# Scores behind values, and the gate products of two tiles in one go, in a fused attention and expert kernel

## The chip, the core and the metric

The kernel runs on one core of a Trainium2 chip. The metric is the time of one execution on the device, in microseconds (us); smaller is better. The program is one launch, and the tensors lie in device memory before it starts and after it ends.

## What is computed

Three stages follow each other: attention within chunks of 64 positions, a dense layer pair with a clipped activation, and a layer of 8 experts of which each token uses two. The token order of the second and third stage is batch, position; their width of 512 is 8 heads of 64. Cut to what matters:

```python
# q, k, v: (4, 8, 576, 64); chunks of 64 positions, so 9 chunks for each head
scores = q_c @ k_c.T / 8
attn = exp(scores - scores.max(-1)); attn /= attn.sum(-1) + 1e-9
x = (attn @ v_c) -> (2304 tokens, 512)

h = x @ w_in                              # 512 -> 2048
x = (h * clip(h + 3, 0, 6) / 6) @ w_out   # 2048 -> 512

logits = x @ w_gate + log1p(exp(x @ w_noise)) * noise      # 8 experts
top2 = the two largest; weights = softmax over the two
out[token] = sum over its two experts: weight * (relu(x @ w1[e]) @ w2[e])   # 512 -> 1024 -> 512
```

Everything is fp32 in and out. The large products are made exact enough by splitting each operand into a rounded high part and a low rest; three matmuls (high by high, high by low, low by high) stand for one.

## The kernel before

The 2304 tokens are 18 tiles of 128. The dense stage takes them in five blocks of 4, 3, 4, 4 and 3 tiles, and goes through 16 weight units for each block. In the profile's times block 0 ends at about 124 us, block 1 at 203, block 2 at 302 and block 3 at 398; the change is in blocks 1, 2 and 3.

Within a unit `u` TensorE (PE) does first S1 (L294: 12 matmuls, the input by this unit's `w_in`, one column for each token of the block) and then S2 of the unit before it (L304: 3 matmuls for each tile of the block that is added up). Between S1 and S2 of the same unit lie two operations of ScalarE (ACT) and two of VectorE (DVE), which make the clipped activation and split it (L329, L330, L331, L336). A unit of S2 thus has the length of one S1 and one S2 as slack.

Besides these matmuls a block carries small work for its neighbours:

- attention for the tiles of the block after it. For one tile: scores on PE (`att_sc`, L197, 16 products of 64x64, shown as 32 matmuls), maximum and subtraction on DVE (L205, L211), exponential on ACT (L223), sum and normalisation on DVE (L228 to L235), transposes on PE (`att_pt`, L247), a copy on ACT (L251), values on PE (`att_xo`, L264, again 16 products of 64x64), and the split into high and low (L274 on ACT, L277 on DVE).
- the gate for the tiles of the block before it. For one tile: four reads of its rows from device memory into `xq` (`gate_l`, L380, issued by SyncE, SP), a transposition on DVE (`gate_d`, L372), a product with the gate weights on PE (`gate_mm`, L413), a copy on ACT (`gate_lp`, L418), a transpose on PE (`gate_rt`, L425) and a sum on DVE (`gate_rr`, L432). After all tiles of a block follow the choice of two experts and the positions.

Scores, transposes and values of attention use the middle 512 columns of a pair of PSUM banks (`middle`, 256 columns in each bank); the gate uses the two outer strips of 256 (`ENDS`) in blocks 2 and 3, and a bank of its own (`p5`) in block 1, where only three tiles are added up.

The order on PE, DVE and ACT is written out by hand: `between` makes lists of what is done at which unit, `at(B, u, f, t)` puts f behind the activation of unit u, and `s1_(u, k, ...)` and `s2_(u, k, ...)` put it behind the k-th third of S1 or the k-th tile of S2 on PE. DVE and ACT get their instructions in the order in which this code issues them, and each engine does them strictly in that order. SP, which issues all plain transfers, is not in that list: a scheduler orders its queue by its own estimates, and SP too goes through it in order.

A further piece of SP's queue: `zero_out` (L739) fills the output and a part of the table `x2d` with zeros: five transfers of 1536 KB that SP issues. It is called in unit 8 of block 2, but the scheduler places it in SP's queue early in block 1, since it waits for little.

The tiles `xq` come from a pool of three buffers (tag `x2`), which is also where the block's results (`x2`) lie until they are written to `x2d`. `gate_d` writes into a fixed tile, `at_[1]`.

Of the kernel before, what the change touches and what calls it, by code (L numbers as in the profile page):

```python
# [8 lines left out]
F32 = mybir.dt.float32  # L9
# [4 lines left out]
AF = mybir.ActivationFunctionType  # L14
ALU = mybir.AluOpType
# [4 lines left out]
P = 128  # L20
NT = 2304
DM = 512
KD = DM // P
# [5 lines left out]
B0 = [sum(BT[:b]) for b in range(len(BT))]  # L29
# [23 lines left out]
def tile_kernel(ctx, tc, qkv, w1u, w2u, wg, noise, out):  # L53
# [15 lines left out]
               "p3": (3, 0), "p4": (3, 1)}  # L69

    def middle(pair):
        return pairs[pair][:, 2 * P:6 * P]
# [19 lines left out]
    early = const.tile([P, NE], F32, name="early")  # L92
    quarter = const.tile([P, 1], F32, name="quarter")
    wg_sb = const.tile([P, KD, 32], F32, name="wg_sb")
    lp = const.tile([P, P], F32, name="lp")
    noise_sb = const.tile([P, NTILE, NE], F32, name="noise_sb")
    pay = const.tile([P, NTILE, 2, 2], I32, name="pay")
    cnt = const.tile([P, NE + 1], I32, name="cnt")
# [88 lines left out]

    def att_sc(t, pair=0):  # L190
        qt, kt, vt = st["qkv", t]
        sc = middle(pair).rearrange("p (r h k) -> p r h k", r=2, h=KD)
        for hp in range(KD):
            for c in range(2):
                for r in range(2):
                    s = slice(r * 64, r * 64 + 64)
                    nc.tensor.matmul(sc[c * 64:c * 64 + 64, r, hp, :], qt[s, hp, c, :], kt[s, c, hp, :],  # L197
                                     start=True, stop=True)
        st["sc", t] = sc

    def att_mx(t, acts):
        sc = st["sc", t]
        mx = work.tile([P, 8, 1], F32, tag="mx", bufs=3, name="mx")
        sc = sc.rearrange("p r h k -> p (r h) k")
        nc.vector.tensor_reduce(mx, sc, axis=AX.X, op=ALU.max)  # L205
        sm = (lead[t][:, 3 * DM:] if t < BT[0] else arena[:, 6]).rearrange("p (h k) -> p h k", h=8)
        su = work.tile([P, 8, 1], F32, tag="su", bufs=3, name="su")
        if acts:
            nc.vector.tensor_scalar(mx, mx, -0.125, None, op0=ALU.mult)
        else:  # L210
            nc.vector.tensor_tensor(sm, sc, mx.to_broadcast([P, 8, 64]), op=ALU.subtract)  # L211
            st.pop(("sc", t))
        st["att", t] = (sm, su, mx, acts)

    def att_e(t, heads=range(8)):
        sm, su, mx, acts = st["att", t]
# [25 lines left out]

    def att_pt(t, pair=0):
        sm = st.pop(("att", t))[0].rearrange("p h k -> p (h k)")
        pt = middle(pair)
# [8 lines left out]
    def att_xo(t, pair=0):  # L254
        at = st.pop(("attT", t))
        qt, kt, vt = st.pop(("qkv", t))

        xo = middle(pair).rearrange("p (a j n) -> p a j n", a=2, j=2)
        for c in range(2):
            for j in range(2):  # L260
                for a in range(2):
                    s = slice(a * 64, a * 64 + 64)
                    for r in range(2):
                        nc.tensor.matmul(xo[r * 64:r * 64 + 64, a, j, c * 64:c * 64 + 64], vt[s, c, j, r, :],  # L264
                                         at[s, r * 2 + j, c * 64:c * 64 + 64], start=True, stop=True)
        st["xo", t] = xo
# [113 lines left out]
            nc.sync.dma_start(xq[32 * a:32 * a + 32].rearrange("p (c n) -> p c n", c=KD), rows[a])  # L380
        st["xq", t] = xq

    def gate_d(t, i=1):
        x = at_[i].rearrange("p k n -> p (k n)")
        quarters_t(x, st.pop(("xq", t)))
        st["x2T", t] = x.rearrange("p (c b j) -> p b c j", c=KD, b=KD)

# [14 lines left out]
    ENDS = [pairs[0][:, :2 * P], pairs[0][:, 6 * P:]]  # L402

    def gate_m(t, tag="p6"):
        gate_mm(t, tag)
        gate_lp(t)

    def gate_mm(t, tag="p6"):

        xt = st.pop(("x2T", t))  # L410
        lg = bank(tag, [P, P], "lg")
        for kd in range(KD):
            nc.tensor.matmul(lg[32 * kd:32 * kd + 32].rearrange("p (c j) -> p c j", c=KD), wg_sb[:, kd, :], xt[:, kd],  # L413
                             start=True, stop=True, tile_position=(0, 32 * kd))
        st["lg", t] = lg

    def gate_lp(t):
        nc.scalar.activation(lp, st.pop(("lg", t)), AF.Copy)  # L418

    def gate_r(t, tag="p6"):  # L420
        gate_rt(t, bank(tag, [P, P], "lt"))
        gate_rr(t)

    def gate_rt(t, lt):
        nc.tensor.transpose(lt, lp, ident)  # L425
        st["lt", t] = lt

    def gate_rr(t):
# [3 lines left out]
        nc.vector.tensor_reduce(st["lgs", g][:, t - GRP[g][0], :], st.pop(("lt", t)).rearrange("p (k e) -> p e k", k=KD)[:, :16],  # L432
                                axis=AX.X, op=ALU.add)

    def small(shape, name, dt=F32, bufs=1):
# [337 lines left out]
    def at(d, u, f, *a):  # L773
        d.setdefault(u, []).append((f, *a))
# [10 lines left out]
    def regular(b, side, A={}, B={}, Z={}):  # L785
        nonlocal prev
        for u in range(U1):
            mlp_s1(b, u, gtile(), 0)
            run(Z.get(u, []))
            mlp_act(b, u)  # L790
            run(A.get(u, []))
            for pb, v in prev:
                mlp_o(pb, v)
            mlp_lo(b, u)
            for pb, v in prev:
                if v == U1 - 1:
                    x2_out(pb)
            run(B.get(u, []))
            if b == NB - 1 and u > 0:
                pump()  # L800
            run(side.get(u, []))
            prev = [(b, u)]

    def between(b, attn, gates, top, per):


        A, B, Z, nt, n0 = {}, {}, {}, BT[b], st.get("tick", 0)
        before = BT[b - 1]

        def s2_(u, k, f, *a):  # L810
            n = n0 + 3 + k if u == 0 else n0 + 3 + before + (3 + nt) * (u - 1) + 3 + k
            at(ticks, n, f, *a)

        def s1_(u, k, f, *a):
            n = n0 + k if u == 0 else n0 + 3 + before + (3 + nt) * (u - 1) + k
            at(ticks, n, f, *a)


        for i, u in enumerate(gates):
            t = B0[b - 1] + i  # L820
            at(B, max(u - 2, 0), gate_l, t)
            at(B, u - 1, gate_d, t)
            if nt > 3:
                s2_(u, nt, gate_mm, t)
                at(B, u, gate_lp, t)
                s1_(u + 1, 2, gate_rt, t, ENDS[0][:, P:])
                s1_(u + 1, 2, gate_rr, t)
            else:
                s1_(u + 1, 1, gate_mm, t, "p5")
                at(A, u + 1, gate_lp, t)  # L830
                s1_(u + 2, 1, gate_rt, t, bank("p5", [P, DM], "lt")[:, P:2 * P])
                s1_(u + 2, 1, gate_rr, t)
        for i, u in enumerate(attn):
            t = B0[b + 1] + i
            s2_(u, 1, att_sc, t)
            at(B, u, att_mx, t, False)
            at(B, u, att_e, t)
            at(B, u + 1, att_n, t)
            if nt > 3:
                s1_(u + 2, 3, att_pt, t)  # L840
                at(A, u + 2, att_at, t, at_[0])
                s2_(u + 2, nt, att_xo, t)
                end = (B, u + 2)
            else:
# [12 lines left out]
        at(B, pm, gate_ps, b - 1)  # L857
        return A, B, Z
# [94 lines left out]
    ends = ctx.enter_context(tc.tile_pool(name="ends", bufs=1, space=PSUM, side="right", reuse_waits="tile"))  # L953
    single.update((tag, ends.tile([P, DM], F32, name="b" + tag)) for tag in ("p6", "p7"))
# [139 lines left out]
```

## Time and profile before

| | us |
|---|---|
| three runs | 935.14, 935.76, 937.75 (median 935.76) |
| the profiled execution | 934.58 |
| its span, first to last instruction | 932.8 |
| PE busy in the span | 913.1 |
| DVE busy | 482.2 |
| ACT busy | 333.2 |

Busy PE is not PE at its peak: the records of matmuls overlap. What a piece of PE's work costs is therefore read from starts, from the start of one row of the timeline to the start of the next. All such differences below are made so. DMA sizes in the profile are in KB of 1024 bytes, and a transfer's time to landing is from its issue by SP until its semaphore is set.

### The profile page before, as it was taken

The page shows a single profiled execution, that of the slowest core. Times are in us where ns is not written, and L with a number is a line of the kernel's source. Part 1 is how long each engine was busy: PE and PEld are TensorE (multiplying, and loading weights), DVE is VectorE, ACT ScalarE, POOL GpSimd, SP SyncE. Part 2 cuts the span into 40 slices and gives each one's busy share as a digit, 9 for nine tenths or more (in the row PEclk, how much of TensorE's full clock was granted, in tenths as well). Part 3 has the DMA queues.
Part 4 walks back from the last instruction along what each step waited for, and adds up shares of the span by engine and source line. Part 5 has one row for each costly group of instructions (what it writes and reads, how often), then busy time and mean ns, then how long its engine had stood idle before and what let it go on. Part 6 is the DMA issues. An engine that isn't in the chain of part 4 may idle for free.

```text
span 932.8 us, 14436 instructions
## 1 busy us (share of the span) xinstructions
PE 913.1 (98%) x5814; PEld 766.3 (82%) x5814; DVE 482.2 (52%) x912; ACT 333.2 (36%) x643; POOL 231.9 (25%) x213
## 2 busy tenths in 40 slices
PE   6999999999999999999999999999999999999996
PEld 3677788887777777788988898898988889888885
DVE  6999965454454443537543555444545454441311
ACT  5565433333233322344541443333434333321210
POOL 0000000030002000033203345754645445332321
PEclk9999999999999999999999999999999999999999
DMA  9636639113112410024541764653746355240422
GB/s 342 204 112 193 193 98 372 61 37 101 35 34 58 136 35 1 1 69 113 156 139 15 191 145 116 151 121 113 145 117 128 111 128 127 69 54 20 54 25 33
DMA packets 49916, 101.49 MB, mean 109 GB/s; under 512 B 17040, under 2 KB 23056, under 8 KB 49840
## 3 DMA queue, kind: packets, MB, share of 16 engines
q1 hardware_dynamic: 38736, 80.38, 27.4%
q0 software_dynamic: 11104, 20.10, 11.9%
q8 instruction: 47, 0.77, 0.4%
q14 instruction: 29, 0.24, 0.1%
HBM read 77.66 MB, written 22.75 MB: 108 GB/s over the span
## 4 chain that ended last, share of the span: by engine, by line
PE 86%; DVE 10%; ACT 2%; issue 1%; DMA 0%; POOL 0%; POOLq 0%; DVEq 0%; ACTq 0%
PE bp L304 41%; PE bp L294 40%; DVE u L171 2%; DVE u L163 2%; DVE u L162 1%; DVE r L330 1%; DVE w L185 1%; DVE g L336 1%; PE pair L197 1%; PE pair L264 1%; PE pair L247 1%; ACT w L178 1%; PE bp L581 0%; ACT r L329 0%; DMA xr<-x2d,tab 0%
## 5 line engine op out<-in xcount | busy, mean ns | idle before, releaser
L304 PE MATMUL bp<-w,g 128*128 128x512 f32 (+1 forms) x1812 | 453.9, 396 | 0.4 <-ACT g L331 0.3
L304 PEld LDWEIGHTS bp<-w,g 128*128 128x128 f32 (+1 forms) x1812 | 328.3, 185 | 73.7 <-DVE g L336 0.8
L294 PE MATMUL bp<-Xa,w 128*128 128x304 f32 (+3 forms) x1344 | 244.2, 332 | 2.3 <-ACT w L178 1.9
L294 PEld LDWEIGHTS bp<-Xa,w 128*128 128x128 f32 x1344 | 209.0, 188 | 30.4 <-ACT w L178 5.2
L554 POOL DMA_INDIRECT xrq<-x2d,iq x114 | 119.5, 1048 | 95.7 <-DVE iq L548 34.4
L597 DVE SCALAR_TENSOR_TENSOR g<-bp,g 128x304 fp32r<-128x304 f32 (+2 forms) x128 | 60.4, 472 | 130.9 <-ACT g L596 130.9
L139 DVE TENSOR_TENSOR w<-raw,w 128x1024 fp32r<-128x1024 f32 x64 | 78.4, 1226 | 89.0 <-ACT w L138 89.0
L519 POOL DMA_INDIRECT table<-pay,slot x36 | 36.3, 1009 | 338.9 <-DVE slot L516 247.9
L596 ACT ACTIVATE g<-bp 128x304 fp32r<-128x304 f32 (+2 forms) x128 | 54.3, 424 | 168.6 <-PE bp L294 168.5
L294 PE MATMUL bp<-Xb,w 128*128 128x384 f32 (+1 forms) x480 | 106.1, 366 | 0.0
L294 PE MATMUL bp<-Xe,w 128*128 128x304 f32 (+1 forms) x672 | 102.7, 308 | 0.0
L294 PEld LDWEIGHTS bp<-Xe,w 128*128 128x128 f32 x672 | 99.8, 188 | 3.3
L330 DVE SCALAR_TENSOR_TENSOR r<-r,bp 128x512 f32<-128x512 f32 (+1 forms) x80 | 50.6, 632 | 91.8 <-ACT r L329 91.6
L294 PEld LDWEIGHTS bp<-Xb,w 128*128 128x128 f32 x480 | 85.3, 188 | 12.5 <-issue 1.8
L624 POOL DMA_INDIRECT out_dram<-arena,tab x40 | 62.7, 1567 | 123.5 <-DVE arena L621 100.1
L329 ACT ACTIVATE r<-bp,b 128x512 f32<-128x512 f32 (+1 forms) x80 | 51.3, 642 | 106.4 <-PE bp L294 106.4
L138 ACT ACTIVATE w<-raw 128x1024 fp32r<-128x1024 f32 x64 | 67.7, 1058 | 58.8 <-PE bp L304 58.5
L336 DVE TENSOR_TENSOR g<-r,g 128x512 fp32r<-128x512 f32 (+1 forms) x80 | 51.0, 637 | 40.2 <-ACT g L331 40.2
L331 ACT ACTIVATE g<-r 128x512 fp32r<-128x512 f32 (+1 forms) x80 | 47.2, 590 | 60.3 <-DVE r L330 60.3
L178 ACT ACTIVATE w<-u 128x512 fp32r<-128x512 f32 x32 | 20.3, 633 | 32.5 <-DVE u L171 32.5
L372 DVE STREAM_TRANSPOSE arena<-xrq 128x512 f32<-128x512 f32 (+1 forms) x30 | 31.4, 1046 | 0.1
L735 POOL MEMSET zero<- 128x1024 f32 x1 | 1.0, 952 | 115.1 <-DVE u L171 115.1
(148 smaller groups left out, 483.8 us busy)
## 6 DMA issues: line engine op xcount, KB each, us to landing
raw<-in_w2u_dram SPq DMA_DIRECT2D x64, 512.0 KB, 4.0
raw<-in_w1u_dram SPq DMA_DIRECT2D x24, 512.0 KB, 4.9
arena<-in_qkv_dram SPq DMA_DIRECT2D x14, 768.0 KB, 4.1
out_dram<-zero SPq DMA_DIRECT2D x4, 1536.0 KB, 19.4
rawx<-in_w1u_dram SPq DMA_DIRECT2D x8, 512.0 KB, 8.4
x2d<-x SPq DMA_DIRECT2D x15, 256.0 KB, 3.4
xq<-x2d SPq DMA_DIRECT2D x44, 64.0 KB, 3.4
xrq<-x2d,iq POOLq DMA_INDIRECT x114, 2.6
```

The costliest lines, as they stand in the source:

```text
L138: nc.scalar.activation(w[:, 0], raw, AF.Copy)
L139: nc.vector.tensor_tensor(w[:, 1], raw, w[:, 0].bitcast(F32), op=ALU.subtract)
L294: nc.tensor.matmul(dst, w[:, a, kd * P:(kd + 1) * P], x[:, b, kd, t0:t0 + n], start=(k == 0), stop=(k == 3 * KD - 1))
L304: nc.tensor.matmul(acc[i][:gi.shape[2]], gi[:, a], w[:, b, DM:], start=(first and j == 0), stop=(last and j == 2))
L329: nc.scalar.activation(r, st["h", b], AF.Relu, bias=b3)
L330: nc.vector.scalar_tensor_tensor(r, r, 6.0, st["h", b], op0=ALU.min, op1=ALU.mult)
L331: nc.scalar.activation(st["g", b, u][:, 0], r, AF.Copy)
L336: nc.vector.tensor_tensor(g[:, 1], st["r", b], g[:, 0].bitcast(F32), op=ALU.subtract)
L554: nc.gpsimd.indirect_dma_start(out=xr[:, c * P:(c + 1) * P], out_offset=None, in_=x2q, in_offset=bass.IndirectOffsetOnAxis(ap=st["iq", key ...
L596: nc.scalar.activation(g[:, 0, t0:t0 + n], h, AF.Relu)
L597: nc.vector.scalar_tensor_tensor(g[:, 1, t0:t0 + n], h, 0.0, g[:, 0, t0:t0 + n].bitcast(F32), op0=ALU.max, op1=ALU.subtract)
L624: s = nc.gpsimd.indirect_dma_start(out=out, out_offset=bass.IndirectOffsetOnAxis(ap=tab[:n, i, 0:1], axis=0), in_=y, in_offset=None, compu ...
```

## The change

Scores get a place of their own, the two outer strips of the pair (`outer`), so that they can follow the values of the tile before directly. The two operations on DVE that read them take a view of two strips. In blocks 1 to 3 attention starts every 3 (block 1) or 2 units (blocks 2 and 3), so that the values of one tile and the scores of the next but one step fall on the same place. The gate takes a list of one or two tiles: products of both, one copy, transposes of both, one sum. `gate_d` writes a tile from the pool `x2` in place of `at_[1]`. The tables at the end set the units.

```diff
+    def outer(pair):
+        return pairs[pair].rearrange("p (r n) -> p r n", r=4)[:, ::3]
...
-    lp = const.tile([P, P], F32, name="lp")
+    lp = const.tile([P, 2 * P], F32, name="lp")
...
-    def att_sc(t, pair=0):
+    def att_sc(t, pair=0, place=middle):
         qt, kt, vt = st["qkv", t]
-        sc = middle(pair).rearrange("p (r h k) -> p r h k", r=2, h=KD)
+        sc = place(pair).rearrange("p r (h k) -> p r h k", h=KD)
...
-    def gate_d(t, i=1):
-        x = at_[i].rearrange("p k n -> p (k n)")
+    def gate_d(t):
+        x = work.tile([P, DM], F32, tag="x2", bufs=3, name="xT")
         quarters_t(x, st.pop(("xq", t)))
...
+    def gate_mm(ts, lg):
+        for i, t in enumerate(ts):
+            xt = st.pop(("x2T", t))
+            for kd in range(KD):
+                nc.tensor.matmul(lg[32 * kd:32 * kd + 32, i * P:(i + 1) * P].rearrange("p (c j) -> p c j", c=KD),
+                                 wg_sb[:, kd, :], xt[:, kd], start=True, stop=True, tile_position=(0, 32 * kd))
+        st["lg", ts[0]] = lg[:, :len(ts) * P]
+
+    def gate_lp(ts):
+        nc.scalar.activation(lp[:, :len(ts) * P], st.pop(("lg", ts[0])), AF.Copy)
...
+    def gate_rt(ts, lt):
+        for i in range(len(ts)):
+            nc.tensor.transpose(lt[:, i * P:(i + 1) * P], lp[:, i * P:(i + 1) * P], ident)
+        st["lt", ts[0]] = lt[:, :len(ts) * P]
...
-        for i, u in enumerate(gates):
-            t = B0[b - 1] + i
-            at(B, max(u - 2, 0), gate_l, t)
-            at(B, u - 1, gate_d, t)
+        first = B0[b - 1]
+        for u, n in gates:
+            ts = list(range(first, first + n))
+            first += n
+            for i, t in enumerate(ts):
+                at(B, u - n - 1 + i, gate_l, t)
+                at(B, u - n + i, gate_d, t)
             if nt > 3:
-                s2_(u, nt, gate_mm, t)
-                at(B, u, gate_lp, t)
-                s1_(u + 1, 2, gate_rt, t, ENDS[0][:, P:])
-                s1_(u + 1, 2, gate_rr, t)
+                s2_(u, nt, gate_mm, ts, ENDS[0])
+                at(B, u, gate_lp, ts)
+                s1_(u + 1, 2, gate_rt, ts, ENDS[1])
+                s1_(u + 1, 2, gate_rr, ts)
             else:
-                s1_(u + 1, 1, gate_mm, t, "p5")
...
+                p5 = bank("p5", [P, DM], "lg")
+                s1_(u + 1, 1, gate_mm, ts, p5)
...
         for i, u in enumerate(attn):
             t = B0[b + 1] + i
-            s2_(u, 1, att_sc, t)
+            if nt > 3:
+                s2_(u, nt, att_sc, t, 0, outer)
+            else:
+                s1_(u, 2, att_sc, t, 0, outer)
...
-        regular(1, {}, *between(1, (1, 4, 8, 12), (3, 5, 7, 9), 11, 2))
+        regular(1, {}, *between(1, (1, 4, 7, 10), ((4, 2), (8, 2)), 11, 2))
...
-        regular(2, side, *between(2, (1, 4, 8, 12), (5, 7, 9), 10, 2))
+        regular(2, side, *between(2, (1, 3, 5, 7), ((4, 2), (8, 1)), 10, 2))
...
-        regular(3, side, *between(3, (2, 6, 11), (3, 5, 7, 9), 10, 1))
+        regular(3, side, *between(3, (1, 3, 5), ((4, 2), (8, 2)), 10, 1))
```

What this does on PE in block 1, units 4 and 5. Before (`bp4`, `bp3` take S1; `bp0`, `bp1`, `bp2` take S2; `pair0` the attention; `bp5` the gate):

```order
L294 MATMUL bp4_428<-Xb_99,w_586 128x384 x4
L413 MATMUL bp5_424<-at1_101,wg_sb_87 32x128 x4
L294 MATMUL bp4_428<-Xb_99,w_586 128x384 x4
L264 MATMUL pair0_72<-at0_100,arena_94 64x64 x16
L294 MATMUL bp4_428<-Xb_99,w_586 128x384 x4
L304 MATMUL bp0_425<-w_536,g_1442 128x512 x3
L197 MATMUL pair0_72<-arena_94 64x64 x16
L304 MATMUL bp1_426<-w_536,g_1442 128x512 x3
L304 MATMUL bp2_423<-w_536,g_1442 128x512 x3
L294 MATMUL bp3_427<-Xb_99,w_656 128x384 x4
L425 MATMUL bp5_424<-ident_78,lp_88 128x128
L294 MATMUL bp3_427<-Xb_99,w_656 128x384 x8
```

The same place with the change (lines are numbered anew: 297 is S1, 307 S2, 267 the values, 200 the scores, 415 the gate product):

```order
L297 MATMUL bp4_428<-Xb_99,w_586 128x384 x8
L267 MATMUL pair0_72<-at0_100,arena_94 64x64 x16
L200 MATMUL pair0_72<-arena_94 64x64 x16
L297 MATMUL bp4_428<-Xb_99,w_586 128x384 x4
L307 MATMUL bp0_425<-w_536,g_1448 128x512 x3
L307 MATMUL bp1_426<-w_536,g_1448 128x512 x3
L307 MATMUL bp2_423<-w_536,g_1448 128x512 x3
L297 MATMUL bp3_427<-Xb_99,w_656 128x384 x4
L415 MATMUL bp5_424<-xT_1437,wg_sb_87 32x128 x4
L415 MATMUL bp5_424<-xT_1479,wg_sb_87 32x128 x4
L297 MATMUL bp3_427<-Xb_99,w_656 128x384 x8
```

The scores moved behind the values, the first tile's gate product moved from unit 4 to unit 5, and the second tile's stands right behind it.

On DVE, units 2 to 4 of block 1, before (`at1` from `xq_1400` is `gate_d` of the first tile; `r` and `g` belong to S1 and S2):

```order
L372 STREAM_TRANSPOSE at1_101<-xq_1400 128x512
L228 TENSOR_REDUCE su_1407<-arena_94 128x8
L229 TENSOR_SCALAR su_1407<-su_1407 128x8
L230 RECIPROCAL su_1407<-su_1407 128x8
L235 TENSOR_TENSOR arena_94<-arena_94,su_1407 128x512
L330 SCALAR_TENSOR_TENSOR r_1455<-r_1455,bp3_427 128x384
L336 TENSOR_TENSOR g_1442<-r_1455,g_1442 128x384
L277 TENSOR_TENSOR Xa_95<-pair0_72,Xa_95 128x2x2x128
L330 SCALAR_TENSOR_TENSOR r_1515<-r_1515,bp4_428 128x384
```

With the change:

```order
L375 STREAM_TRANSPOSE xT_1437<-xq_1400 128x512
L231 TENSOR_REDUCE su_1407<-arena_94 128x8
L232 TENSOR_SCALAR su_1407<-su_1407 128x8
L233 RECIPROCAL su_1407<-su_1407 128x8
L238 TENSOR_TENSOR arena_94<-arena_94,su_1407 128x512
L333 SCALAR_TENSOR_TENSOR r_1461<-r_1461,bp3_427 128x384
L339 TENSOR_TENSOR g_1448<-r_1461,g_1448 128x384
L375 STREAM_TRANSPOSE xT_1479<-xq_1439 128x512
L280 TENSOR_TENSOR Xa_95<-pair0_72,Xa_95 128x2x2x128
L333 SCALAR_TENSOR_TENSOR r_1530<-r_1530,bp4_428 128x384
```

The transposition of the second tile (`xq_1439`) now stands one row behind unit 3's split, ahead of unit 4's activation.

On SP, from the writing of block 0's results on, before (`xq` with its numbers are the four tiles of block 0, `zero` the fill):

```order
L360 DMA x2d_76<-x2e_1354 128x512
L380 DMA xq_1400<-x2d_76 32x4x128 x4
L380 DMA xq_1473<-x2d_76 32x4x128 x4
L380 DMA xq_1582<-x2d_76 32x4x128 x4
L739 DMA x2d_76<-zero_2491 384x1x1024
L739 DMA out_0_dram<-zero_2491 128x3x1024 x4
L380 DMA xq_1677<-x2d_76 32x4x128 x4
L119 DMA arena_94<-in_qkv_dram 128x1536 x4
```

With the change:

```order
L363 DMA x2d_76<-x2e_1354 128x512
L383 DMA xq_1400<-x2d_76 32x4x128 x4
L745 DMA x2d_76<-zero_2550 384x1x1024
L745 DMA out_0_dram<-zero_2550 128x3x1024 x4
L383 DMA xq_1439<-x2d_76 32x4x128 x4
L122 DMA arena_94<-in_qkv_dram 128x1536
L383 DMA xq_1585<-x2d_76 32x4x128 x4
L383 DMA xq_1631<-x2d_76 32x4x128 x4
```

The reads of the second tile moved from ahead of the five fills to behind them, and the fills moved up by eight reads.

## Rows read from the trace of the kernel before

**Rows 1.** Profile page: busy time of the span, and the chain by engine.
```profile
PE 913.1 (98%) x5814; PEld 766.3 (82%) x5814; DVE 482.2 (52%) x912; ACT 333.2 (36%) x643; POOL 231.9 (25%) x213
...
PE 86%; DVE 10%; ACT 2%; issue 1%; DMA 0%; POOL 0%; POOLq 0%; DVEq 0%; ACTq 0%
```

**Rows 2.** Timeline of PE, block 1: start us, busy us, line, tiles, shape.
```profile
133.79 2.25 PE L294 MATMUL bp<-Xb,w 128*128 128x384 f32 x12
135.88 2.25 PE L304 MATMUL bp<-w,g 128*128 128x512 f32 x9
...
143.14 0.86 PE L294 MATMUL bp<-Xb,w 128*128 128x384 f32 x4
...
146.62 0.85 PE L304 MATMUL bp<-w,g 128*128 128x512 f32 x3
147.40 0.69 PE L197 MATMUL pair<-arena 64*64 64x64 f32 x32
148.03 1.67 PE L304 MATMUL bp<-w,g 128*128 128x512 f32 x6
149.53 0.86 PE L294 MATMUL bp<-Xb,w 128*128 128x384 f32 x4
150.23 0.27 PE L425 MATMUL bp<-ident,lp 128*128 128x128 f32 x1
150.25 1.64 PE L294 MATMUL bp<-Xb,w 128*128 128x384 f32 x8
151.73 2.25 PE L304 MATMUL bp<-w,g 128*128 128x512 f32 x9
153.81 0.86 PE L294 MATMUL bp<-Xb,w 128*128 128x384 f32 x4
154.61 0.42 PE L413 MATMUL bp<-at,wg_sb 128*32 128x128 f32 x8
154.96 1.66 PE L294 MATMUL bp<-Xb,w 128*128 128x384 f32 x8
156.46 0.85 PE L304 MATMUL bp<-w,g 128*128 128x512 f32 x3
```

**Rows 3.** Timeline of PE at the start: two tiles' scores in a row.
```profile
10.13 1.16 PE L197 MATMUL pair<-lead 64*64 64x64 f32 x64
```

**Rows 4.** Timeline of SP in block 1: issues, start and length of each stretch.
```profile
130.63 5.74 SPq L380 DMA_DIRECT2D xq<-x2d  x12
136.47 1.71 SPq L739 DMA_DIRECT2D x2d<-zero  x1
138.22 4.51 SPq L739 DMA_DIRECT2D out_dram<-zero  x4
142.83 7.95 SPq L380 DMA_DIRECT2D xq<-x2d  x4
```

**Rows 5.** Profile page, DMA issues: engine, count, KB each, us to landing.
```profile
out_dram<-zero SPq DMA_DIRECT2D x4, 1536.0 KB, 19.4
```

**Rows 6.** DMA packets by size, first from 143 to 158 us, then from 158 to 162.
```profile
DMA packets 1504, 5.98 MB, mean 398 GB/s; under 512 B 48, under 2 KB 48, under 8 KB 1503
...
DMA packets 756, 1.15 MB, mean 287 GB/s; under 512 B 80, under 2 KB 592, under 8 KB 756
```

**Rows 7.** Timeline of DVE in block 1: start us, busy us, line, operation.
```profile
138.37 1.10 DVE L372 STREAM_TRANSPOSE at<-xq 128x512 f32<-128x512 f32 x1
...
142.26 0.56 DVE L336 TENSOR_TENSOR g<-r,g 128x384 fp32r<-128x384 f32 x1 [0.59 <-ACT g L331]
...
169.25 1.08 DVE L372 STREAM_TRANSPOSE at<-xq 128x512 f32<-128x512 f32 x1
```

**Rows 8.** Windows after PE's last matmul: busy PE, PEld, DVE, ACT, POOL, clock, DMA.
```profile
923.80:928.60 4.80, 0.00 (x0) 0.00 (x0) 0.75 (x1) 0.00 (x0) 2.66 (x2) 1.00 0.67 80
928.70:932.80 4.10, 0.00 (x0) 0.00 (x0) 0.00 (x0) 0.00 (x0) 0.00 (x0) 0.50 0.17 31
```

**Rows 9.** Timeline of PE, the first matmuls of the program.
```profile
1.07 3.17 PE L679 MATMUL pair<-ones 128*128 128x512 bf16 x7 [1.07 <-DVE early L704]
4.27 1.13 PE L197 MATMUL pair<-lead 64*64 64x64 f32 x32
```

More of the change, by code (lines that the diff above doesn't have):

```diff
@@ L71, in middle @@
     def middle(pair):
-        return pairs[pair][:, 2 * P:6 * P]
+        return pairs[pair][:, 2 * P:6 * P].rearrange("p (r n) -> p r n", r=2)
+    def outer(pair):
+        return pairs[pair].rearrange("p (r n) -> p r n", r=4)[:, ::3]
     def bank(tag, shape, name):
@@ L202, in att_mx @@
         sc = st["sc", t]
-        mx = work.tile([P, 8, 1], F32, tag="mx", bufs=3, name="mx")
-        sc = sc.rearrange("p r h k -> p (r h) k")
+        mx = work.tile([P, 2, KD, 1], F32, tag="mx", bufs=3, name="mx")
         nc.vector.tensor_reduce(mx, sc, axis=AX.X, op=ALU.max)
@@ L210, in att_mx @@
         else:
-            nc.vector.tensor_tensor(sm, sc, mx.to_broadcast([P, 8, 64]), op=ALU.subtract)
+            nc.vector.tensor_tensor(sm.rearrange("p (r h) k -> p r h k", r=2), sc, mx.to_broadcast([P, 2, KD, 64]),
+                                    op=ALU.subtract)
             st.pop(("sc", t))
-        st["att", t] = (sm, su, mx, acts)
+        st["att", t] = (sm, su, mx.rearrange("p r h o -> p (r h) o"), acts)
     def att_e(t, heads=range(8)):
@@ L244, in att_pt @@
         sm = st.pop(("att", t))[0].rearrange("p h k -> p (h k)")
-        pt = middle(pair)
+        pt = middle(pair).rearrange("p r n -> p (r n)")
         for m in range(KD):
@@ L256, in att_xo @@
         qt, kt, vt = st.pop(("qkv", t))
-        xo = middle(pair).rearrange("p (a j n) -> p a j n", a=2, j=2)
+        xo = middle(pair).rearrange("p a (j n) -> p a j n", j=2)
         for c in range(2):
@@ L404, in gate_m, with gate_rr @@
     def gate_m(t, tag="p6"):
[L405 to L418, printed above, removed]
-    def gate_r(t, tag="p6"):
[L421 to L428, printed above, removed]
+        gate_mm([t], bank(tag, [P, P], "lg"))
+        gate_lp([t])
+    def gate_mm(ts, lg):
[7 more added lines that the diff above has]
+        nc.scalar.activation(lp[:, :len(ts) * P], st.pop(("lg", ts[0])), AF.Copy)
+    def gate_r(t, tag="p6"):
+        gate_rt([t], bank(tag, [P, P], "lt"))
+        gate_rr([t])
+    def gate_rt(ts, lt):
+        for i in range(len(ts)):
+            nc.tensor.transpose(lt[:, i * P:(i + 1) * P], lp[:, i * P:(i + 1) * P], ident)
+        st["lt", ts[0]] = lt[:, :len(ts) * P]
+    def gate_rr(ts):
+        t, n = ts[0], len(ts)
         g = max(i for i in range(len(GRP)) if GRP[i][0] <= t)
@@ L431, in gate_rr @@
             st["lgs", g] = small([P, 5, 16], "lgs")
-        nc.vector.tensor_reduce(st["lgs", g][:, t - GRP[g][0], :], st.pop(("lt", t)).rearrange("p (k e) -> p e k", k=KD)[:, :16],
+        i = t - GRP[g][0]
+        nc.vector.tensor_reduce(st["lgs", g][:, i:i + n, :],
+                                st.pop(("lt", t)).rearrange("p (t k e) -> p t e k", t=n, k=KD)[:, :, :16],
                                 axis=AX.X, op=ALU.add)
@@ L816, in s1_ @@
             at(ticks, n, f, *a)
-        for i, u in enumerate(gates):
-            t = B0[b - 1] + i
-            at(B, max(u - 2, 0), gate_l, t)
-            at(B, u - 1, gate_d, t)
+        first = B0[b - 1]
[5 more added lines that the diff above has]
+                at(B, u - n + i, gate_d, t)
             if nt > 3:
-                s2_(u, nt, gate_mm, t)
-                at(B, u, gate_lp, t)
-                s1_(u + 1, 2, gate_rt, t, ENDS[0][:, P:])
-                s1_(u + 1, 2, gate_rr, t)
-            else:
-                s1_(u + 1, 1, gate_mm, t, "p5")
-                at(A, u + 1, gate_lp, t)
-                s1_(u + 2, 1, gate_rt, t, bank("p5", [P, DM], "lt")[:, P:2 * P])
-                s1_(u + 2, 1, gate_rr, t)
+                s2_(u, nt, gate_mm, ts, ENDS[0])
+                at(B, u, gate_lp, ts)
+                s1_(u + 1, 2, gate_rt, ts, ENDS[1])
+                s1_(u + 1, 2, gate_rr, ts)
+            else:
+                p5 = bank("p5", [P, DM], "lg")
+                s1_(u + 1, 1, gate_mm, ts, p5)
+                at(A, u + 1, gate_lp, ts)
+                s1_(u + 2, 1, gate_rt, ts, p5[:, 2 * P:])
+                s1_(u + 2, 1, gate_rr, ts)
         for i, u in enumerate(attn):
             t = B0[b + 1] + i
-            s2_(u, 1, att_sc, t)
+            if nt > 3:
+                s2_(u, nt, att_sc, t, 0, outer)
+            else:
+                s1_(u, 2, att_sc, t, 0, outer)
             at(B, u, att_mx, t, False)
```

## The prediction

> **What bounds the kernel now.** I read the page first: PE is busy for 913 of 932.8 us and makes 86% of the chain that ended last [rows 1]. So two kinds of things count: PE time taken out, and any wait put into PE's queue. Then I read PE's timeline from start to start, in block 1, where plain and interrupted stretches stand near each other [rows 2]. A plain S1 there takes 135.88 - 133.79 = 2.09 us, a plain S2 of three tiles 153.81 - 151.73 = 2.08 us. The reader is to see that a small product between them costs more than its own rows: the matmuls before and behind it are late too. Last I read SP's queue and the DMA, since the order shows a move there [rows 4 to 6].
>
> **What the merging on PE saves.** S2 with scores inside runs from 146.62 to 149.53, 2.91 us; against 2.08 that is 0.83 us for one separate group of scores. Inside a run a second tile's scores cost less: two tiles in a row were busy 1.16 us where one is 0.69, so 0.47 us more [rows 2, 3]. A group of scores that moves right behind values, which have the same 64x64 shape, saves 0.83 - 0.47 = 0.36 us. Of the 11 tiles in blocks 1 to 3, the first of each block stays alone, so 8 move: 8 x 0.36 = 2.9 us. Bounds: nothing, if values and scores do not chain as scores and scores do, and 8 x 0.47 = 3.8.
>
> A gate product alone: S1 with one inside runs from 153.81 to 156.46, 2.65 us, 0.56 over 2.09. Two in a row are nowhere in these rows. The second costs at most 0.56 (no gain), and at least 0.12, a quarter of the 0.47 that 32 matmuls took, for 8 with wider outputs. I take 0.20, near the lower end, because a second 64x64 group also cost only its steady part. Each of 5 merges (11 tiles become 6 groups) then saves 0.36: 1.8 us, between 0 and 2.2. A gate transpose inside S1 costs 151.73 - 149.53 - 2.09 = 0.11 us, which is what one transpose takes; pairing them I put at 0, between 0 and 5 x 0.11. The wider copy on ACT and the wider sum on DVE lie on engines that are busy 36% and 52%, with one S1 and one S2 of slack, as do maximum and subtraction from two strips: 0, and at most a few tenths. The part on PE is -4.7 us, between 0 and -6.5.
>
> **What the order of SP adds.** Here the change does something that its PE rows do not show. The five fills were queued behind the reads of three tiles; now they stand ahead of the second tile's. Before, 12 reads took 5.74 us to issue, 0.48 each, and the first fill was issued at 136.47 [rows 4]. With 8 reads fewer ahead it is issued 8 x 0.48 = 3.8 us earlier, at 132.6.
>
> What a read costs behind the fills the trace of before shows, because the fourth tile's reads stood there. They were issued between 142.83 and 150.78 [rows 4]. From 143 to 158 us the DMA engines moved 398 GB/s, and no packet of at least 512 bytes and under 2 KB was among them (48 and 48 in the two cumulative counts); from 158 to 162 there were 592 - 80 = 512 such packets, exactly one tile's 4 x 128 rows of 512 bytes [rows 6]. So these reads ran only when the fills had ended, some 11 to 15 us after their issue; the last fill itself landed 19.4 us after its issue [rows 5]. It cost nothing: that tile is transposed at 169.25 [rows 7].
>
> Now the second tile has that place. Everything shifted by 3.8, its reads run from 154.2 to 158.2, and its transposition, 1.10 us, ends at 159.3. DVE reaches it right behind unit 3's split, which before began at 142.26 and ended at 142.8 [rows 7]. DVE goes in order, so behind it wait the low part of the values and the activation of unit 4. PE goes on until it needs something of this. From S1 of unit 4, which starts at 143.14: S1 2.09, values and scores 0.83 + 0.47, S2 2.08, then four matmuls of S1 of unit 5, 0.70 (149.53 to 150.23, the same piece), and the gate product of the first tile, 0.2. That is 149.5. The next matmul is the gate product of the second tile, and it waits until 159.3: **9.8 us** of standing PE. Bounds: 0, if small reads pass the fills, and 12.8, if the reads need a whole 4 us after the last fill has landed. (That fill was issued at about 142.73 - 4.51 / 4 = 141.6, so at 137.8 now; 137.8 + 19.4 + 4 + 1.1 = 162.3.)
>
> **What comes after the wait.** DVE has a unit's work to make up, and PE may be slow. The clock after PE's last matmul is 1.00 for 4.8 us and then 0.50, which is 1.2 in place of 2.4 GHz [rows 8]. PE would stand longer than that here, 9.8 us. At the program's start the first seven matmuls of 512 columns took 3.20 us, 0.457 each [rows 9], where 9 of 512 columns now take 2.08, 0.231 each: 1.6 us lost over that stretch alone. Bounds: 0 (the clock stays and DVE's slack suffices) and 4.2 (a whole unit, 2.09 + 2.08, is lost). I take **2.5**, since rows 9 end before the clock had risen; DVE's catching up lies beside the slow matmuls.
>
> By rows alone it is open whether the clock falls in the middle of the kernel too: they show the fall at its end. The Trainium skill, "TensorE: Matmul & The Clock Gate" (Part 1: The HAM clock gate), says that the throttled clock is the default and only sustained work releases it. By that rule it falls here for certain and the sum is at least 934.58 - 4.7 + 9.8 + 1.6 = 941.3; if it stayed, 939.7 and what DVE owes.
>
> The later tiles of the gate are not hit: the third and fourth are needed in unit 8, well after the fills, and blocks 2 and 3 have no such fill. The first transposes of attention and the choice of experts keep their units, and so what they cost.
>
> **The sum.** 934.58 - 2.9 - 1.8 + 9.8 + 2.5 = 942.2 us for the profiled execution. The median of the three runs lies 1.2 above it, the lowest 0.6; I forecast between, **942.7 us**.
>
> **Rivals.**
> 1. The reads pass the fills, and only the saving is left. What it needs: the second tile landed by 147 or so, so that DVE's wait stays within the slack. For it: 64 KB of reads is little, and one transfer is spread over 16 engines. Against it: the fourth tile before, in the same place in the same queue, did not pass. The time would be 934.6 to 935.8 less 4.7, 930 to 931. Faster. The Trainium skill, "DMA: Bandwidth & Descriptors" (Queues, rings and completion order), says that completion is not in order for the transfers of one issuing engine, though each ring is consumed in order. Rows 6 speak against reading this as a way past the fills.
> 2. The wait comes, but is shorter than 5 us, because the fill starts later than SP's order lets it or PE finds more to do. For it: the fill waits for a memory set on POOL. Against it: SP issued the first fill right at the end of the reads (130.63 + 5.74 = 136.37, then 136.47), so it waited for nothing. 935 to 938.
> 3. The change does not do what it says: values and scores do not chain, or each moved group costs the same 0.83 in its new place. Then 934.6 + 9.8 + 2.5 = 946.9. For it: no row shows values followed by scores. Against it: the shape is the same.
> 4. The wait spreads: the stop makes reads of later tiles and attention inputs late, which stand behind it in SP's queue, and a second stop follows in units 6 to 8. 947 to 951. Against it: by then the DMA is idle and SP has units of time.
>
> **How the numbers follow.** The forecast's mechanism 0.70, rival 1 0.10, rival 2 0.07, rival 3 0.07, rival 4 0.06. The forecast's own range is 939 to 946: the saving from -3 to -6.5, the wait from 8.5 to 11.5, what follows from 0.5 to 4, not all at one end. With parts of rivals 2 to 4, **937 to 948** holds the time 8 times in 10. About 0.3%, 2.8 us, is what a measurement here can tell from no change, so up to 938.6 counts as the same. Slower by more: 0.70 + 0.07 + 0.06 = 0.83; within: rival 2, 0.07; faster: rival 1, 0.10.
>
> **What would show it right or wrong.** In the new profile PE has one long idle stretch before the gate product of block 1, line 415, released by DVE's transposition, line 375, at about 150 to 159 us; DVE idles before that transposition, released by the DMA of `xq`; the granted clock falls to 0.5 near the end of that stretch. The fills are issued near 132.6. Scores stand right behind values, two rows of 32 matmuls that start about half a microsecond apart, and gate products come in rows of 16. From 170 us to the end of block 3 the new kernel gains on the old, some 3 us by the plain difference of starts. Wrong would be: no idle stretch there, or reads of the second tile ahead of the fill's last packets.

## The result and the profile after

Time after: 943.30 us median of 5 runs (941.32 to 943.76); the kernel before, run on the same chip, 935.29 (934.45 to 937.75). The ratio is 1.0078, with a 95% interval of 1.006 to 1.0095: slower by 0.78%, which is 7.3 us (the two medians lie 8.0 apart). The forecast was 942.7 us. The profiled execution took 942.81 us, with a span of 941.0; set against the one of before this is +8.23.

Waits of PE, the kernel after: line waited for and its releaser, us in total, times, longest. In the kernel before the first is not there, the second is 0.6 us, once, and the third 0.4, once.

```profile
PE bp L415 <- DVE xT L375: 8.8, 1, 8.8
...
PE pair L267 <- ACT at L254: 1.1, 2, 0.6
PE pair L250 <- DVE arena L238: 0.8, 3, 0.4
```

The first row is the wait that was forecast: the gate product of the second tile, for VectorE's transposition of it. Of the second row 0.5 us, and of the third two of the three places, are new; the forecast put them at nothing, and they come up below.

Timeline of PE around it: start us, busy us, line, tiles, shape, and in brackets the idle time before and its releaser. It answers [rows 2].

```profile
143.43 1.56 PE L297 MATMUL bp<-Xb,w 128*128 128x384 f32 x8
144.91 0.69 PE L267 MATMUL pair<-at,arena 64*64 64x64 f32 x32
145.43 0.65 PE L200 MATMUL pair<-arena 64*64 64x64 f32 x32
146.00 0.97 PE L297 MATMUL bp<-Xb,w 128*128 128x384 f32 x4
146.81 2.25 PE L307 MATMUL bp<-w,g 128*128 128x512 f32 x9
148.89 0.86 PE L297 MATMUL bp<-Xb,w 128*128 128x384 f32 x4
149.69 0.43 PE L415 MATMUL bp<-xT,wg_sb 128*32 128x128 f32 x8
158.89 0.66 PE L415 MATMUL bp<-xT,wg_sb 128*32 128x128 f32 x8 [8.78 <-DVE xT L375]
159.47 2.93 PE L297 MATMUL bp<-Xb,w 128*128 128x384 f32 x8
162.20 2.37 PE L307 MATMUL bp<-w,g 128*128 128x512 f32 x9
164.41 0.86 PE L297 MATMUL bp<-Xb,w 128*128 128x384 f32 x4
```

Values and scores start 145.43 - 144.91 = 0.52 us apart, and S1 with both takes 146.81 - 143.43 = 3.38, 1.29 over a plain one, where the sum had 1.30 (0.83 + 0.47). The two gate products start 9.20 us apart. Behind them the rest of S1 takes 162.20 - 159.47 = 2.73 us, where it is 1.50 [rows 2]; the S2 that follows takes 164.41 - 162.20 = 2.21, 0.12 over a plain one.

Timeline of SP in block 1, and of DVE: they answer [rows 4] and [rows 7].

```profile
130.91 1.92 SPq L383 DMA_DIRECT2D xq<-x2d  x4
132.87 0.65 SPq L745 DMA_DIRECT2D x2d<-zero  x1
133.56 4.51 SPq L745 DMA_DIRECT2D out_dram<-zero  x4
138.12 9.33 SPq L383 DMA_DIRECT2D xq<-x2d  x4
```

```profile
142.53 0.56 DVE L339 TENSOR_TENSOR g<-r,g 128x384 fp32r<-128x384 f32 x1 [0.59 <-ACT g L334]
157.75 1.08 DVE L375 STREAM_TRANSPOSE xT<-xq 128x512 f32<-128x512 f32 x1 [14.66 <-DMA xq<-x2d]
158.76 0.65 DVE L280 TENSOR_TENSOR Xa<-pair,Xa 128x512 fp32r<-128x512 f32 x1
```

The first fill is issued at 132.87, 3.6 us earlier than before; the four reads behind the fills are issued by 138.12 + 9.33 = 147.45, and VectorE stands 14.66 us for them. Packets of the DMA engines from 138 to 154 us, and from 154 to 158 (the counts under 512 B and under 2 KB are cumulative), as in [rows 6]:

```profile
DMA packets 1588, 6.25 MB, mean 391 GB/s; under 512 B 64, under 2 KB 64, under 8 KB 1587
...
DMA packets 817, 1.17 MB, mean 292 GB/s; under 512 B 93, under 2 KB 666, under 8 KB 817
```

No packet of 512 bytes up to 2 KB in the first stretch, 666 - 93 = 573 in the second; one tile has 512. The reads ran when the fills had ended, in the 4 us that the forecast gave them.

Windows of the stretch: busy us of PE, PEld, DVE, ACT and POOL, the granted clock, DMA share, GB/s.

```profile
150.00:152.00 2.00, 0.11 (x5) 0.00 (x0) 0.00 (x0) 0.00 (x0) 0.00 (x0) 1.00 1.02 410
152.00:154.00 2.00, 0.00 (x0) 0.00 (x0) 0.00 (x0) 0.00 (x0) 0.00 (x0) 0.54 1.03 295
...
160.00:162.00 2.00, 2.00 (x8) 2.00 (x7) 1.51 (x3) 0.42 (x1) 0.00 (x0) 0.50 0.17 44
162.00:164.00 2.00, 2.00 (x10) 1.68 (x9) 0.83 (x2) 1.10 (x2) 0.00 (x0) 0.90 0.34 98
```

The clock falls to 0.5 (1.2 GHz) while PE stands, and not near the end of that stretch, as the forecast had it, but by about 152.2 us: 0.54 from 152 to 154. It is back at 2.4 GHz early in the last window. The Trainium skill, "TensorE: Matmul & The Clock Gate" (Part 1: The HAM clock gate), has the throttled clock as the default that sustained work releases; by that the clock had to fall here, and the 0.54 agrees.

From unit to unit, against the kernel before, block 1 is 9.2 us longer, block 2 is 1.1 shorter and block 3 0.6 shorter; all that lies behind block 3 takes 0.4 us more together, all that lies ahead of block 1 0.3.

### The profile page after: what moved, and what is told of

Read it like the earlier page. It is cut to its first block, busy times and chain, and to the rows that moved or that the text cites. A ratio compares the mean times of both kernels' runs of the same rounds, so it can differ in the third digit from the quotient of the medians.

```text
span 941.0 us, 14426 instructions
## 1 busy us (share of the span) xinstructions
PE 909.5 (97%) x5814; PEld 767.7 (82%) x5814; DVE 481.5 (51%) x907; ACT 331.5 (35%) x638; POOL 230.4 (24%) x213
```

## The experiments

The times of a run are put against the kernel before on the same chip. The first four ran on a chip on which the kernel before took 945.25 us, and where PE pauses between 557 and 608 us in every trace, the one with the order of before included. So beside the ratio stands the length of blocks 1 to 3 in the trace, from the first S1 of block 1 to that of block 4, which lies ahead of these pauses: 397.62 - 123.92 = 273.70 us before, 405.42 - 124.19 = 281.23 after. For the other runs it is the same difference of starts.

### The fills behind the reads

```diff
-        nc.gpsimd.memset(zero, 0.0)
+        nc.vector.memset(zero, 0.0)
```

The fills now follow VectorE's order, which has the memory set in unit 8 of block 2, and SP issues them at 261.8 us.

> The kernel after the change, with the memory set of the zero tile on VectorE in place of GpSimd; so the five fills stand in SP's order behind all sixteen reads of block 1's gate, and nothing else on PE or ScalarE moves. Theory (the reads of the second tile waited behind the fills): the wait of 9.2 us before the gate product in block 1 is gone, with it the 1.2 us of slow matmuls behind it and the 0.5 us before the values of the next unit: 943.3 - 10.9 = 932.4, between 931 and 934. Rival (the two transpositions of VectorE in one go, or the denser order on PE, make the wait, and the place of the fills does not matter): 942 to 944, with a wait of several us still before that gate product.

Measured: ratio 0.9969 (0.9951 to 0.9987), 2.9 us less than before, which at the level of the first measurement is 932.4. Blocks 1 to 3 take 270.71 us, 3.0 less than before and 10.5 less than after. PE's timeline:

```profile
149.31 0.65 PE L415 MATMUL bp<-xT,wg_sb 128*32 128x128 f32 x16
149.89 1.67 PE L297 MATMUL bp<-Xb,w 128*128 128x384 f32 x8
151.40 2.26 PE L307 MATMUL bp<-w,g 128*128 128x512 f32 x9
```

Both gate products run in one row of sixteen at 149.31, where the kernel after stopped at 150.1, and S1 behind them takes 151.40 - 149.89 = 1.51. The place of the fills is the whole cause of the stop; the order on PE is untouched here, and gains. One expectation missed: the 0.5 us before the values stays, so it has nothing to do with the fills. PE, and ScalarE ahead of it:

```profile
189.87 0.69 PE L267 MATMUL pair<-at,arena 64*64 64x64 f32 x32 [0.44 <-ACT at L254]
```

```profile
188.81 0.53 ACT L334 ACTIVATE g<-r 128x384 fp32r<-128x384 f32 x1 [2.19 <-DVE r L333]
189.24 0.58 ACT L254 ACTIVATE at<-pair 128x512 f32<-128x512 f32 x1
```

These are the values of the last tile whose attention block 1 carries, which the new table puts two units earlier (units 10 to 13, where it had been 12 to 15). ScalarE's copy `at` comes late, since it stands behind an activation that waits 2.19 us for VectorE. There the choice of experts, which keeps its units 11 and 12, now lies on VectorE between this tile's scaling and the next activation: from 185.44 to 188.25 us. In the kernel before, that activation follows the scaling directly.

The same edit in the kernel before:

> The kernel before, with the same memory set on VectorE, so its fills too stand behind all sixteen reads. Theory: PE waited nowhere for these fills in the kernel before, so there is nothing to gain: 935.3, between 934.3 and 936.3. Rival (fills in block 1 disturb the kernel wherever they stand, by the DMA traffic itself): at least 2 us faster, 933 or less, and then the gain of the run beside this one is not the order of the reads.

Measured: ratio 1.0006 (0.999 to 1.0023). The late fill gains nothing where nobody waits for reads behind it, and the rival's 2 us are outside the interval. (Its trace has blocks 1 to 3 at 276.01, 2.3 more; that arose in the first two units of block 2 and the first of block 3, not around the fills, and stays open.)

### The fills ahead of all reads, in the kernel before

```diff
-        regular(1, {}, *between(1, (1, 4, 8, 12), (3, 5, 7, 9), 11, 2))
...
-        at(side, 8, zero_out)
+        at(side, 0, zero_out)
+        regular(1, side, *between(1, (1, 4, 8, 12), (3, 5, 7, 9), 11, 2))
+        side = {}
```

> The kernel before, merging nothing, with the zero fills moved ahead of all sixteen reads of block 1's gate in SP's order. Theory (reads behind fills make PE wait, in any order on PE): the first tile's reads land near 155.5; VectorE's transposition of it stands ahead of the scaling that the transposes of attention need at 140.7, so PE stands there until about 158, 17 us, and the clock costs 1 to 2 more: 952 to 955 beside 935.3, 17 to 20 us more. Rival (only the merged order on PE and the two transpositions together turn late reads into a wait): 935 to 938.

Measured: ratio 1.0194 (1.0177 to 1.0211), 952.07 us beside 933.81, 18.3 more. Blocks 1 to 3 take 292.22. SP, then DVE, then PE:

```profile
130.16 0.65 SPq L739 DMA_DIRECT2D x2d<-zero  x1
130.86 4.85 SPq L739 DMA_DIRECT2D out_dram<-zero  x4
135.75 21.86 SPq L380 DMA_DIRECT2D xq<-x2d  x16
```

```profile
154.77 1.08 DVE L372 STREAM_TRANSPOSE at<-xq 128x512 f32<-128x512 f32 x1 [16.51 <-DMA xq<-x2d]
```

```profile
157.64 1.11 PE L247 MATMUL pair<-ident,arena 128*128 128x128 f32 x4 [16.93 <-DVE arena L235]
```

The first tile's reads landed by 154.8, when its transposition starts (155.5 expected), and PE stood for 16.9 us (17 expected) at the transposes of attention, whose scaling stands behind the tile's transposition on VectorE. No merging is needed for the stop; the order in SP's queue makes it.

### The reads through another queue

```diff
-            nc.sync.dma_start(xq[32 * a:32 * a + 32].rearrange("p (c n) -> p c n", c=KD), rows[a])
+            (nc.scalar if t == 1 else nc.sync).dma_start(
+                xq[32 * a:32 * a + 32].rearrange("p (c n) -> p c n", c=KD), rows[a])
```

> The kernel after the change, fills where they are, with the four reads of the second tile alone issued by ScalarE in place of SyncE, so through another queue. Theory (the reads were held by their place in SyncE's queue): they run between the packets of the fill, 512 of 512 bytes against fill packets of some 4 KB; at 391 GB/s over 16 engines such a packet takes 0.17 us, and 32 reads on each engine, one after each fill packet, 5.4 us; the tile is there by 146 and the gate's product at 149.3 does not wait. The wait of 9.2, the clock's 1.2 and the 0.5 behind it go, against which four issues on ScalarE put up to 2 us: 932 to 935 beside 943.3, or 8 to 11 us less. Rival (the fill keeps the DMA engines themselves busy, whatever queue the reads stand in): the product still waits until 155 to 159, and the time is 941 to 944.

Measured: ratio 1.0001 (0.9991 to 1.001), 7.2 us below the kernel after by the two ratios, a little under what was expected. Blocks 1 to 3 take 272.59. ScalarE's issue, the DMA issues from 134 to 160 us (KB each, median us to landing), and PE:

```profile
137.02 4.53 ACTq L383 DMA_DIRECT2D xq<-x2d  x4
```

```profile
out_dram<-zero SPq DMA_DIRECT2D x3, 1536.0 KB, 19.5
...
xq<-x2d SPq DMA_DIRECT2D x8, 64.0 KB, 3.4
xq<-x2d ACTq DMA_DIRECT2D x4, 64.0 KB, 8.3
```

```profile
149.67 0.43 PE L415 MATMUL bp<-xT,wg_sb 128*32 128x128 f32 x8 [0.21 <-DVE xT L375]
...
155.74 0.44 PE L428 MATMUL bp<-ident,lp 128*128 128x128 f32 x2 [1.26 <-ACT lp L420]
```

Fills and reads are in flight at once, and the reads land 8.3 us after their issue, in the middle of the fill. So it was the place in SP's queue that held the reads back for the whole of the fills. The fills' own traffic still costs something: 8.3 us to landing, beside 3.4 for the reads that SP issues later. The Trainium skill, "DMA: Bandwidth & Descriptors" (Queues, rings and completion order), has each ring consumed in order; this run agrees. The tile still came 4.5 us late for VectorE. The delay cost 0.4 us at the gate's product and 1.5 at its transposes (1.26 of it idle), by the starts beside those of the run with the fills late, and the expectation missed both.

### What follows the wait

```diff
+            if ts[0] == 0 and i == 0 and len(ts) == 2:
+                for _ in range(75):
+                    nc.tensor.matmul(bank("p5", [P, DM], "lt")[:, 2 * P:].rearrange("p (a n) -> p a n", a=2),
+                                     ones, ones[:, None, :].to_broadcast([P, 2, P]), start=True, stop=True)
```

> The kernel after the change, with 75 matmuls of 256 columns (of ones, their result read by nobody) between the gate products of the first and the second tile in block 1, some 8 us of work in the stretch in which TensorE stood. Theory (the 1.2 us lost behind the wait are the granted clock): the clock stays at 1.00 there, the rest of S1 behind the products takes 1.5 us in place of 2.73, and the time is 1.3 lower than after the change, 942.0 beside 943.3. Rival (they are VectorE making up its delay): the rest of S1 stays at 2.7 and the time at 943.3, at either clock.

Measured: ratio 1.0087 (1.007 to 1.0104), no less than the kernel after. Blocks 1 to 3 take 281.73. PE, and a window of the stretch:

```profile
149.82 8.36 PE L419 MATMUL bp<-ones 128*128 128x256 bf16 x75
159.24 0.42 PE L415 MATMUL bp<-xT,wg_sb 128*32 128x128 f32 x8 [1.06 <-DVE xT L375]
159.60 1.68 PE L297 MATMUL bp<-Xb,w 128*128 128x384 f32 x8
161.11 2.24 PE L307 MATMUL bp<-w,g 128*128 128x512 f32 x9
163.19 0.86 PE L297 MATMUL bp<-Xb,w 128*128 128x384 f32 x4
165.30 0.44 PE L432 MATMUL bp<-ident,lp 128*128 128x128 f32 x2 [1.25 <-ACT lp L424]
```

```profile
156.00:158.00 2.00, 2.00 (x20) 1.70 (x18) 0.00 (x0) 0.00 (x0) 0.00 (x0) 1.00 0.97 284
```

Half of each account holds. The clock stayed at 1.00 and S1 behind the products took 1.51, so the slow matmuls were the clock. But the time did not come back: PE, being fast, now reached the transposes 1.25 us before ScalarE's copy, which is late because VectorE is. The reads landed a little later too: the transposition starts 34.13 us after the first S1 of block 1, and 33.56 in the kernel after. With these 0.57 taken off, block 1 is 0.07 shorter than in the kernel after, so keeping the clock gains nothing. Two more runs looked at this: the transposes of that pair moved one S1 later, with the 75 matmuls and without.

```diff
-                s1_(u + 2, 1, gate_rt, ts, p5[:, 2 * P:])
-                s1_(u + 2, 1, gate_rr, ts)
+                s1_(u + 2 + (u == 4), 1, gate_rt, ts, p5[:, 2 * P:])
+                s1_(u + 2 + (u == 4), 1, gate_rr, ts)
```

> The run with 75 matmuls in the stretch of the wait, and the transposes of the first gate pair one S1 later (unit 7 in place of 6), so that ScalarE and VectorE have two units to make up their delay. Theory now (after the wait two limits lie beside each other, the clock at half and the delay of VectorE and ScalarE, each worth about 1.4 us alone): here neither is left, the wait of 1.25 us at those transposes goes and block 1 is 1.4 us shorter than in the run with the 75 matmuls, time 1.4 less, ratio 1.0072. Rival (the delay stays whole and stands at the next thing that PE needs from VectorE, the transposes of attention or the values): no less time, ratio 1.0087.

Measured: ratio 1.0075 (1.0058 to 1.0092), not told apart from 1.0087; blocks 1 to 3 take 281.51, 0.2 less and not 1.4, and by 0.2 the reads landed earlier. The wait moved on to the next thing that PE needs from VectorE, the transposes of attention:

```profile
167.19 0.66 PE L250 MATMUL pair<-ident,arena 128*128 128x128 f32 x4 [1.23 <-DVE arena L238]
```

The rival was right here: giving one step more room does not shorten the delay of VectorE and ScalarE.

> The kernel after the change, with only the transposes of the first gate pair one S1 later. Theory now (either limit alone costs 1.4): the clock still falls in the wait, S1 behind it still takes 2.7 us, and nothing is gained: ratio 1.0078. Rival (the delay of the other engines is the real limit and the clock hides in it): 1.2 to 1.4 us less, ratio 1.0064.

Measured: ratio 1.008 (1.0058 to 1.0102), blocks 1 to 3 281.79, no gain; S1 behind the wait takes 162.09 - 159.37 = 2.72 us, nearly the 2.73 of the kernel after. Blocks 1 to 3 are 0.56 longer than there: the reads landed 0.2 later, and the S2 that follows takes 2.57 us in place of 2.21, since the clock came back later (0.73 from 162 to 164 us, where it was 0.90). So at half clock the slow matmuls cost 1.35 to 1.7 us and the delay hides in them; at full clock the delay costs 1.2 us of idle time, some 1.5 by starts, and shows as a wait.

### The gates one tile at a time, and attention first

Both start from the run with the fills late.

```diff
-        regular(1, {}, *between(1, (1, 4, 7, 10), ((4, 2), (8, 2)), 11, 2))
+        regular(1, {}, *between(1, (1, 4, 7, 10), ((3, 1), (5, 1), (7, 1), (9, 1)), 11, 2))
...
-        regular(2, side, *between(2, (1, 3, 5, 7), ((4, 2), (8, 1)), 10, 2))
+        regular(2, side, *between(2, (1, 3, 5, 7), ((4, 1), (6, 1), (8, 1)), 10, 2))
...
-        regular(3, side, *between(3, (1, 3, 5), ((4, 2), (8, 2)), 10, 1))
+        regular(3, side, *between(3, (1, 3, 5), ((2, 1), (4, 1), (6, 1), (8, 1)), 10, 1))
```

> The run with the fills late, but with the gates of blocks 1 to 3 one tile at a time again (at units 3, 5, 7, 9; 4, 6, 8; 2, 4, 6, 8), while scores stay behind values. Theory: five pairs come apart, at 0.35 us each that is 1.8 us more on PE; the waits of transposes of attention for VectorE in blocks 2 and 3 (1.2 us in three places), which came with two transpositions in one unit, go: 0.6 us slower than the run with the fills late, 0 to 2. Rival A (pairing the gate saves nothing): 1.2 us faster than that run. Rival B (the waits of the transposes are the attention's own places and not the gate's): they stay, and it is 1.8 us slower.

Measured: ratio 0.999 (0.9972 to 1.0009), 0.2% over the run with the fills late. Blocks 1 to 3 take 273.40, 2.7 us more, beyond the range. By blocks it is 1.2, 0.0 and 1.5. In block 2 one pair came apart and one wait of 0.4 went, and they cancel, as the theory has it. The excess is from where I had put the single gates, most of it one new wait in block 3:

```profile
318.60 2.14 PE L297 MATMUL bp<-Xb,w 128*128 128x512 f32 x8
...
320.86 1.17 PE L297 MATMUL bp<-Xb,w 128*128 128x512 f32 x4
323.23 0.66 PE L250 MATMUL pair<-ident,arena 128*128 128x128 f32 x4 [1.20 <-DVE lgs L437]
```

Here the gate's sum, `lgs`, stands ahead of the scaling on VectorE and has to wait for the gate's transposes on PE. From start to start that S1 takes 323.23 - 318.60 = 4.63 us, where the next S1 with a single gate transpose takes 3.01: 1.6 more. In block 1 an S2 with the transposes of attention takes 3.0 in place of 2.5. With these, 0.35 a pair fits: block 1 2 x 0.35 + 0.5 = 1.2; block 3, where two waits of the run with the fills late go (0.83, below), 2 x 0.35 - 0.83 + 1.6 = 1.5. Rival A is out. The S1 behind a pair starts 0.57 us after the products, and 0.36 after a single one, so the second product costs 0.21 us (0.23 in block 1), as estimated.

The whole loop over `attn` (scores, maximum, scaling, values) moves ahead of the loop over `gates`:

```diff
+        for i, u in enumerate(attn):
+            t = B0[b + 1] + i
...
         first = B0[b - 1]
         for u, n in gates:
...
-        for i, u in enumerate(attn):
-            t = B0[b + 1] + i
```

> The run with the fills late, with the steps of attention put ahead of those of the gate within a unit, so that on VectorE the scaling of the arena goes ahead of the transpositions that share its unit. Theory: the transposes of attention wait no more behind a gate's transposition; four places, 0.4 + 0.4 + 0.3 + 0.5 = 1.6 us less than the run with the fills late, about 930.8. Rival (the transposes' matmuls are late for another reason, or the gate's product becomes late instead): within 0.5 us of that run, and the waits of the transposes are still there or stand at a gate product.

Measured: ratio 0.9925 (0.9905 to 0.9944). Blocks 1 to 3 take 268.93, 4.8 less than before and 1.8 less than with the fills late alone. What it removes is seen in block 2 of the kernel after; DVE, then PE:

```profile
229.71 1.07 DVE L375 STREAM_TRANSPOSE xT<-xq 128x512 f32<-128x512 f32 x1
230.71 0.64 DVE L231 TENSOR_REDUCE su<-arena 128x8 f32<-128x512 f32 x1
...
231.83 0.69 DVE L238 TENSOR_TENSOR arena<-arena,su 128x512 f32<-128x512 f32 x1
```

```profile
229.53 2.88 PE L297 MATMUL bp<-Xa,w 128*128 128x512 f32 x12
232.57 0.65 PE L250 MATMUL pair<-ident,arena 128*128 128x128 f32 x4 [0.17 <-DVE arena L238]
```

The scaling is issued behind a transposition that nobody needs until two units later, and PE meets it late: 232.57 - 229.53 = 3.04 us, where such an S1 takes 2.72 without the wait, and a slower group of transposes, 0.38 in all by the plain difference. Three such places are new with the change (0.38 here, 0.33 and 0.50 in block 3), one in block 1 is old (0.57, of which 0.36 is idle time); in this run none is left.

> The run with fills late and attention first once more. Its trace was 4.9 us ahead of the kernel before at the start of block 4, while its time stood at 0.9925 of it, 7.1 us. Theory: the gain is what the trace shows by block 4, ratio 0.9948, and the 2 us beyond it were the scatter of runs on that chip. Rival: there is a further gain behind block 4, and the ratio is 0.9925 again.

Measured: 929.87 us beside 933.81, ratio 0.9953 (0.9936 to 0.997), blocks 1 to 3 again 268.93. That is the theory's 0.9948, and the excess of the first measurement did not come back on another chip, with the same blocks 1 to 3; that it was scatter fits, though the two intervals overlap. By the ratios this version is faster than both kernels: by 0.5% than the one before, by 1.2% than the one after.

## Why the prediction was right

The mechanism was right and its largest term nearly exact; two smaller ones were off, and it was luck that their errors cancelled.

- **The order of SP and the wait.** Fills 3.6 us earlier (3.8 forecast), reads run from 154 to 158 (154.2 to 158.2), transposition ended at 158.8 (159.3), 9.2 us of standing PE (9.8). That the reads stand behind the fills is shown three ways: taken away (10.5 us back), done alone (16.9 us of wait), and by another queue (through in 8.3 us). What carried it was a tile of the kernel before that already stood behind the fills at no cost [rows 4, 6].
- **After the wait.** Forecast 2.5, measured 2.73 - 1.50 + 0.12 = 1.35. That is even under the 1.6 that the forecast put as the least with a fallen clock. It had taken more since rows 9 end before the clock had risen; here the clock was back 3.5 us after PE resumed, with 1.23 us lost over eight matmuls of 384 columns and 0.12 behind them. VectorE's delay did lie beside the slow matmuls. Keeping the clock gains nothing, which the forecast left open. The forecast also took the clock to last longer from [rows 8] than it did; that changed no term.
- **The saving on PE.** Forecast 4.7, and by the run with the fills late and attention first, 273.70 - 268.93 = 4.8 by blocks 1 to 3. That includes the old wait of 0.57 that attention first removes and still holds the new one of 0.5 at line 267, so they nearly cancel. From unit 8 of block 1 to the end of block 3 the kernel after gains 2.8 on the one before, as the forecast had it (some 3).
- **The step that failed** is "The first transposes of attention and the choice of experts keep their units, and so what they cost", which put VectorE's new order at nothing. The gate's transpositions, which now go in twos, stand ahead of the scaling for the first transposes of blocks 2 and 3 and the last of block 3 (1.2 us in three places). The choice of experts keeps its units, but the last tile that block 1 does attention for has moved into them, and its values wait for ScalarE (0.5). Of the saving of 4.7 so only 3.0 reach the kernel after.

With these sizes: -4.7 + 1.7 + 9.2 + 1.35 = 7.55, against 281.23 - 273.70 = 7.53 in blocks 1 to 3; the 0.7 left to the 8.23 of the executions lies ahead of and behind them, where the change moves nothing. Errors of -0.6, -1.15 and +1.7 cancelled by luck, so the time agreed better than its terms. One reading was loose: the 19.4 us of [rows 5] are the median of the four fills of the output, not the last one's; only the upper bound of the wait used them.

Rival 1 (reads pass the fills) is excluded in one queue and holds through another. Rival 2 fell with the wait's size, rival 3 with the 0.52 between values and scores, rival 4 with the lack of a second long wait.

## What to carry to other kernels

Where an edit moves work on one engine, read what it moves in the queues of the others: here a small read that fell behind large transfers in its queue waited for all of them, and one that did so already, at no cost, gave the price. After the long stop here, the clock and the delay of the other engines lay beside each other; removing one showed the other. A step that nobody needs for two units does not belong ahead of one that TensorE needs in the same unit.

## What the runs showed of the hardware

- The issue itself took longer behind the fills: four reads took SP 1.92 us with no fill ahead and 9.33 us behind the fills, and the profile shows no wait of SP in those 9.33; four on ScalarE's queue beside the fills took 4.53.
- The granted clock was still 1.00 in the 4.8 us behind PE's last matmul [rows 8], but 0.54 from 152 to 154 us in the kernel after, when PE had stood since 150.1. It rose again while PE ran the slow S1 and S2.
- On the chip of the first four runs the same kernel before took 945.25 us, with a spread of 7.6, beside 933.81 and 934.76 on two others; PE paused in the experts' stage with no releaser in the profile. What caused this is open.
